# Bound rows read from the accumulator through a picking product; query scalings and unhurried norm applications on GpSimd

## The chip, the core and the metric

The kernel runs on one core of a Trainium2 chip. The metric is device time in microseconds (us) of one execution. A core has five engines that run their own instruction streams and wait for each other through semaphores: TensorE (PE, matrix products into PSUM; PEld is its weight load), ScalarE (ACT, activation functions), VectorE (DVE), GpSimd (POOL) and SyncE (SP, which issues the transfers).

## The reference: what is computed

Two transformer layers over 2048 tokens of width 512, each an attention with 32 heads of width 16, and a feed-forward block of width 1376. The layers share their weights.

```python
def _A_ref(x, wqkv, wo):            # attention, H = 32, Dh = 16
    qkv = ...(x @ wqkv)...
    scores = jnp.einsum("bhqd,bhkd->bhqk", q, k) * Dh ** -0.5
    p = _softmax(scores, axis=-1)
    o = jnp.einsum("bhqk,bhkd->bhqd", p, v)
    return (...o...) @ wo

def _B_ref(x, w1, b1, w2, b2):      # feed-forward, F = 1376
    y = _layernorm(x, axis=-1)
    h = _gelu(jnp.einsum("bsd,df->bsf", y, w1) + b1)
    return jnp.einsum("bsf,fd->bsd", h, w2) + b2

x = A_x                              # (1, 2048, 512)
x = x + _A_ref(_layernorm(x), A_wqkv, A_wo)
x = x + _B_ref(_layernorm(x), B_w1, B_b1, B_w2, B_b2)
x = x + _A_ref(_layernorm(x), A_wqkv, A_wo)
x = x + _B_ref(_layernorm(x), B_w1, B_b1, B_w2, B_b2)
```

## The kernel before

The kernel is a Python program that makes a static schedule: jobs (generators) hand in tasks for an engine, a list scheduler with a duration for every task puts them in order, and the order found is emitted as five instruction streams. The code's layer numbers are 1 and 3.

Attention is cut into 88 *segments*. A segment is one group of four heads (`hg`, 8 of them) and one group of query tokens (512 wide, the last two groups of the second layer 256). A segment's work is score tiles of 128 keys x 512 queries for each head. The first query group of each layer is split into two segments by key blocks (`nparts == 2`), so that it can begin before all keys are there: 32 segments are of this kind. In the first eight segments (the narrow stage) only ACT takes the exponentials.

The exponential of a score is taken with a bound instead of the row maximum. The bound stands in row 16 of each head's 32 rows in the query block `QT`, which is made by one multiply-and-add with a scale per row and a bias:

```python
def job_qt(self, sg, s):
    q = yield ("get", "qt")                       # one of three query slots
    yield ("keys", [("scl", L, part)])
    yield Task("dve", 0.4, [I(lambda e: e.tensor_scalar(out=self.QT[:, q, 0:W], in0=src,
        scalar1=self.scl[:, k, hg:hg + 1], scalar2=self.qbias[:, 0:1], op0=ALU.mult, op1=ALU.add), ...)])
    ...
```

The exponential of a tile is taken in one of two ways. ACT takes groups of three and two tiles with its Exp. DVE takes single tiles: it converts the score to an integer whose bits are a bf16 power of two (`d_load`), and three added shifts of it, multiplied by four scaled copies of the values, make up the exponential:

```python
def d_load(self, d):                              # L1466: PSUM to integer bits
    ... Task("dve", 0.0, [I(lambda e: e.tensor_scalar(out=self.dp[:, u, w * 512:(w + 1) * 512],
            in0=self.ps[:, b, :], scalar1=BITS0, scalar2=None, op0=ALU.add), ...)])

def job_d(self, bt):                              # L1497: three shifts for two tiles
    for k in range(1, len(SHIFT)):
        yield Task("dve", pr, [I(lambda e, k=k, v=v: e.tensor_scalar(out=self.dp[:, v, 0:N],
            in0=self.dp[:, u, 0:N], scalar1=float(SHIFT[k]), scalar2=None, op0=ALU.add), ...)])
```

Which tiles DVE takes is not fixed. Five of the sixteen key blocks (`DK`) may go to it, and `take_d` gives it one when its queue is short; what it does not take goes to ACT:

```python
def take_d(self, hps):
    if ... self.dload > 1 or P.free["dve"] - S_.now > 1.3 or sum(o[4] for t in S_.pend["dve"] for o in t.ops) > DBACK:
        return None
    if self.batch is None and (not S_.pools["dp"].free or ... or self.flying >= DFLY):
        return None
    ...
```

The products with the values are accumulated in one PSUM bank, `ACCB`, 17 rows for each of four heads (16 values and the sum). At a segment's end DVE transposes the bank. For a split segment the two parts have different bounds, so their bounds are needed too: DVE transposes the query block for it.

```python
def job_segend(self, sg):
    yield Task("dve", 0.3, [... e.transpose(self.accT[:, a, 0:W], self.ps[:, ACCB, 0:W]) ...])     # L1593
    T = self.accT[:, a, 0:W].rearrange("p (b r) -> p b r", r=32)
    if nparts == 2:
        xs = yield ("get", "xn")
        rowT = self.xn[:, xs, :].rearrange("p (b r) -> p b r", r=32)
        yield Task("dve", 1.2, [... e.transpose(self.xn[:, xs, :], self.QT[:, q, :]) ...])         # L1602
    S_.release("qt", q)
    if nparts == 2 and part == 0:
        yield Task("dve", 1.2, [... e.tensor_copy(out=self.rowA[:, hg, :], in_=rowT[:, :, 16]) ...])
        ...                                       # GpSimd keeps values and sums of part 0
        return
    if nparts == 2:
        yield Task("dve", 1.2, [... e.tensor_tensor(out=dw, in0=rowT[:, :, 16], in1=self.rowA[:, hg, :], op=ALU.subtract) ...])
        yield Task("act", -1.0, [... exp of dw ...])
        yield Task("pool", 1.2, [... part 0 rescaled and added, four tensor_tensor ...])           # L1621 to L1624
    ...
```

A norm takes its statistics on DVE, the inverse root on GpSimd, and is applied on DVE (`xn` has three slots, shared with the transposed query block):

```python
def ln_apply(self, tt, slot, i, dst, dres, prio):
    c = 4 * slot + i
    return Task("dve", prio, [I(lambda e: e.tensor_scalar(out=dst, in0=self.xres[:, tt, :],
        scalar1=self.mv[:, c, 0:1], scalar2=self.rs[:, c:c + 1], op0=ALU.subtract, op1=ALU.mult), ...)])   # L859
```

It is called for the first four tiles of the first layer, for keys and queries of the others (twice for tiles 4 to 15 of the first layer, once in the second), and for the input of the feed-forward blocks. GpSimd also makes the scaled values `vs` of a segment (L1157) and the norms of queries.

After scheduling, gaps of PE are filled with products by zero (`zw`; L1295, L1297, L1299).

Of the kernel before, what the change touches and what calls it, by code (L numbers as in the profile page):

```python
# [511 lines left out]
class Builder:  # L512
# [171 lines left out]
    def build_startup(self):  # L684
# [155 lines left out]

    def ln_group(self, tiles, slot, prio, eps1, eps0):

# [11 lines left out]
        yield Task("pool", prio, [I(lambda e: e.tensor_scalar(out=rs, in0=var, scalar1=eps1, scalar2=eps0, op0=ALU.mult, op1=ALU.add), [("mv", c0 + i) for i in range(n)], [R], 0.2)])  # L854
        yield Task("pool", prio, [I(lambda e: e.tensor_tensor(out=rs, in0=rs, in1=self.cneg[:, 0:n], op=ALU.pow), [R, ("cneg",)], [R], 0.45 + 0.15 * n)])

    def ln_apply(self, tt, slot, i, dst, dres, prio):
        c = 4 * slot + i
        return Task("dve", prio, [I(lambda e: e.tensor_scalar(out=dst, in0=self.xres[:, tt, :], scalar1=self.mv[:, c, 0:1], scalar2=self.rs[:, c:c + 1], op0=ALU.subtract, op1=ALU.mult),  # L859
                                    [("x", tt), ("mv", c), ("rs", slot)], [dres], 0.395, (), "fast")])  # L860
# [263 lines left out]
    def job_qt(self, sg, s):  # L1124
# [6 lines left out]
        src, RS = (self.psbf(self.q0bank)[:, 0:512], ("ps", self.q0bank)) if s is None else (self.qraw[:, s, 0:W], ("qraw", s))  # L1131
        yield Task("dve", 0.4, [I(lambda e: e.tensor_scalar(out=self.QT[:, q, 0:W], in0=src, scalar1=self.scl[:, k, hg:hg + 1], scalar2=self.qbias[:, 0:1], op0=ALU.mult, op1=ALU.add),
                                  [RS, ("scl", k), ("qbias",)], [("qt", q)], 0.16 + 0.24 * W / 512, (), "fast")])
        if s is None:
# [451 lines left out]
    def job_segend(self, sg):  # L1586
# [10 lines left out]
        T = self.accT[:, a, 0:W].rearrange("p (b r) -> p b r", r=32)  # L1597
        if nparts == 2:
            xs = yield ("get", "xn")
            RX = ("xn", xs)  # L1600
            rowT = self.xn[:, xs, :].rearrange("p (b r) -> p b r", r=32)
            yield Task("dve", 1.2, [I(lambda e: e.transpose(self.xn[:, xs, :], self.QT[:, q, :]), [("qt", q)], [RX], 0.68)])  # L1602
        S_.release("qt", q)
# [3 lines left out]
        if nparts == 2 and part == 0:  # L1607
            yield Task("dve", 1.2, [I(lambda e: e.tensor_copy(out=self.rowA[:, hg, :], in_=rowT[:, :, 16]), [RX], [("rowA", hg)], 0.17)])
            S_.release("xn", xs)
            if L == 3:  # L1610
# [4 lines left out]
        if nparts == 2:
            dw = self.dw[:, hg % 2, :]
            RW = ("dw", hg % 2)
            yield Task("dve", 1.2, [I(lambda e: e.tensor_tensor(out=dw, in0=rowT[:, :, 16], in1=self.rowA[:, hg, :], op=ALU.subtract), [RX, ("rowA", hg)], [RW], 0.17)])
            S_.release("xn", xs)
            yield Task("act", -1.0, [I(lambda e: e.activation(out=dw, in_=dw, func=ACTF.Exp, scale=EXPS), [RW], [RW], 0.23)])  # L1620
# [309 lines left out]
```

## Time and profile before

The median of three runs is 1602.28 us (1602.15 to 1602.88). The profiled execution spans 1601.8 us, at full granted TensorE clock throughout.

| what | number |
|---|---|
| DVE score conversions (L1466) | 921 |
| DVE shifts (L1497) | 1410 |
| ACT exponential groups (L1374) | 1283, of 3 tiles (609) or 2 tiles (674) |
| DVE query scalings (L1132) | 88 |
| DVE norm applications (L859) | 74 |
| DVE transposes of the query block (L1602) | 32 |
| GpSimd instructions | 406 |

In a line of the groups, the first part is line, engine, operation and output<-input; after xcount come busy us and mean ns of one, and after the second bar the idle time of the engine just before these instructions with what ended it. Instructions of one engine overlap a little, so the sum of a group's durations exceeds the time that it blocks its engine.

### The profile page before, as it was taken

The numbers are of one execution on the slowest core, as the hardware profiler recorded it, in microseconds if no ns is written. First come the engines' busy times: TensorE is split into PE (matmuls) and PEld (weight loads), VectorE is DVE, ScalarE is ACT, GpSimd is POOL, SyncE is SP. The second block draws the span as 40 slices with busy tenths as digits, with TensorE's granted clock in tenths as the row PEclk, the third lists the DMA queues.
The fourth block names the chain that finished last, engine by engine and source line by source line (L and its number), as shares of the span: only waits on it lengthen the run. The fifth ranks groups of instructions, "written<-read, shape, count | busy, mean of one in ns | idle before, by whom it ended". The sixth has DMA issues, their size and how long they took to land.

```text
span 1601.8 us, 39236 instructions
## 1 busy us (share of the span) xinstructions
PE 1571.1 (98%) x16532; PEld 481.3 (30%) x16532; DVE 1473.8 (92%) x3323; ACT 1535.5 (96%) x1366; POOL 207.0 (13%) x406
## 2 busy tenths in 40 slices
PE   9999999999999999999999999999999999999998
PEld 3222222222222222222222233222222222344454
DVE  7999999999999899989999899999899989998893
ACT  6999999999999999989999989999999999999995
POOL 4464210000200001001211124300000000000000
PEclk9999999999999999999999999999999999999999
DMA  6671011213321122222822232210101100211100
GB/s 168 122 168 63 22 31 31 53 30 76 84 44 46 36 62 80 56 61 77 138 45 64 58 71 67 60 26 21 31 15 37 31 22 18 40 40 40 41 22 20
DMA packets 212464, 88.79 MB, mean 55 GB/s; under 512 B 183835, under 2 KB 206656, under 8 KB 212288
## 3 DMA queue, kind: packets, MB, share of 16 engines
q1 hardware_dynamic: 212288, 86.29, 24.0%
q8 instruction: 129, 2.11, 0.6%
q14 instruction: 47, 0.39, 0.1%
HBM read 34.65 MB, written 19.48 MB: 34 GB/s over the span
## 4 chain that ended last, share of the span: by engine, by line
PE 49%; ACT 28%; DVE 20%; issue 1%; DMA 1%; POOL 1%; POOLq 0%; DVEq 0%
ACT PT L1374 25%; PE ps L1389 17%; PE ps L1563 14%; DVE dp L1466 7%; DVE dp L1497 5%; PE ps L1747 4%; PE ps L1704 4%; PE ps L916 4%; PE ps L1295 3%; ACT h L1739 2%; PE ps L1299 1%; DVE accT L1593 1%; PE ps L1297 1%; DVE st L846 1%; PE ps L1649 1%
## 5 line engine op out<-in xcount | busy, mean ns | idle before, releaser
L1374 ACT ACTIVATE PT<-ps 128x1024 bf16<-128x1024 f32 (+1 forms) x1283 | 1457.1, 1269 | 36.0 <-PE ps L1389 30.1
L1389 PE MATMUL ps<-QT,KT 32*128 32x512 bf16 (+1 forms) x4608 | 672.5, 358 | 11.5 <-DVE dp L1466 2.2
L1466 DVE TENSOR_SCALAR dp<-ps 128x512 uint16<-128x512 f32 x921 | 618.7, 683 | 56.7 <-PE ps L1389 54.0
L1497 DVE TENSOR_SCALAR dp<-dp 128x1024 uint16<-128x1024 uint16 (+1 forms) x1410 | 533.0, 421 | 7.4 <-PE ps L1563 3.3
L1563 PE MATMUL ps<-PT,V 128*17 128x512 bf16 (+1 forms) x3568 | 468.3, 358 | 0.0
L1563 PE MATMUL ps<-dp,vs 128*17 128x512 bf16 (+1 forms) x3120 | 441.0, 357 | 0.7 <-DVE dp L1497 0.6
L1389 PEld LDWEIGHTS ps<-QT,KT 32*128 32x128 bf16 x4608 | 169.9, 91 | 541.8 <-ACT PT L1374 260.4
L1563 PE MATMUL ps<-dp,V 128*17 128x512 bf16 (+1 forms) x1040 | 214.5, 357 | 2.3 <-DVE accT L1593 2.0
L1297 PE MATMUL ps<-zw 32*128 32x444 bf16 (+2 forms) x714 | 197.6, 325 | 0.0
L1563 PEld LDWEIGHTS ps<-dp,vs 128*17 128x17 bf16 x3120 | 110.9, 88 | 125.1 <-issue 100.9
L1563 PEld LDWEIGHTS ps<-PT,V 128*17 128x17 bf16 x3568 | 112.3, 88 | 105.3 <-issue 94.4
L1299 PE MATMUL ps<-zw 128*32 128x448 bf16 (+23 forms) x1621 | 142.6, 318 | 0.7 <-DVE dp L1466 0.6
L1295 PE MATMUL ps<-zw 128*128 128x448 bf16 (+17 forms) x560 | 130.6, 334 | 4.1 <-DVE dp L1466 2.2
L854 POOL TENSOR_SCALAR rs<-mv 128x4 f32<-128x4 f32 (+2 forms) x19 | 6.6, 347 | 879.1 <-DVE mv L847 877.7
L1704 PE MATMUL ps<-yT,wf 128*128 128x512 bf16 (+3 forms) x396 | 103.5, 360 | 1.0 <-DVE yT L1830 0.5
L916 PE MATMUL ps<-wqkv,xnT 128*128 128x512 bf16 x336 | 93.1, 382 | 1.0 <-DVE h L929 0.5
L1157 POOL TENSOR_SCALAR vs<-V 128x340 bf16<-128x340 bf16 (+2 forms) x72 | 60.5, 841 | 139.7 <-PE ps L1563 121.6
L1295 PEld LDWEIGHTS ps<-zw 128*128 128x128 bf16 x560 | 42.9, 98 | 83.5 <-issue 52.7
L1563 PEld LDWEIGHTS ps<-dp,V 128*17 128x17 bf16 x1040 | 51.3, 88 | 53.1 <-issue 28.5
L1728 DVE TENSOR_SCALAR h<-ps,b1c 128x512 bf16<-128x512 f32 (+2 forms) x88 | 62.3, 708 | 1.8 <-PE ps L1704 1.5
L1593 DVE STREAM_TRANSPOSE accT<-ps 128x512 f32<-128x512 f32 (+1 forms) x88 | 58.1, 660 | 6.1 <-PE ps L1563 4.9
L1299 PEld LDWEIGHTS ps<-zw 128*32 128x32 bf16 x1621 | 52.4, 95 | 24.7 <-DVE dp L1466 5.7
(172 smaller groups left out, 903.0 us busy)
## 6 DMA issues: line engine op xcount, KB each, us to landing
vs<-vs_scr SPq DMA_DIRECT2D x56, 255.0 KB, 2.7
wf<-in_B_w_dram SPq DMA_DIRECT2D x90, 128.0 KB, 2.8
q_scr<-qk SPq DMA_DIRECT2D x22, 256.0 KB, 2.4
k_scr<-qk SPq DMA_DIRECT2D x12, 256.0 KB, 2.3
out_dram<-xres SPq DMA_DIRECT2D x16, 128.0 KB, 1.7
vs_scr<-vs SPq DMA_DIRECT2D x8, 255.0 KB, 3.8
xres<-in_A_x_dram SPq DMA_DIRECT2D x7, 256.0 KB, 3.1
v_scr<-vst SPq DMA_DIRECT2D x12, 136.0 KB, 1.8
```

The costliest lines, as they stand in the source:

```text
L916: yield Task("pe", prio, [I(lambda e, c=c: e.matmul(self.ps[:, b, :], lhsT=xnT[:, c, :], rhs=self.wqkv[:, c, which * 512:which * 512 + 512 ...
L1295: fn = lambda e: e.matmul(self.ps[:, b, 0:w], lhsT=self.zw[:, 0:128], rhs=self.zw[:, 0:w], start=st, stop=st, skip_group_check=True)
L1297: fn = lambda e: e.matmul(self.ps[:, b, 0:w], lhsT=self.zw[32 * p:32 * p + 32, 0:128], rhs=self.zw[32 * p:32 * p + 32, 0:w], start=st, sto ...
L1299: fn = lambda e: e.matmul(self.ps[32 * p:32 * p + 32, b, 0:w], lhsT=self.zw[:, 0:32], rhs=self.zw[:, 0:w], start=st, stop=st, skip_group_c ...
L1374: S_.submit(Task("act", 1e-5 * gi, [I(lambda e, pt=pt, n=n, b0=b0: e.activation(out=self.PT[:, pt:pt + n, :], in_=self.ps[:, b0:b0 + n, :] ...
L1389: return [I(lambda e, kb=kb, i=i: e.matmul(self.ps[:, b, i * W:(i + 1) * W], lhsT=self.KT[32 * hp:32 * hp + 32, hg, kb * 128:(kb + 1) * 12 ...
L1466: self.S_.submit(Task("dve", 0.0, [I(lambda e: e.tensor_scalar(out=self.dp[:, u, w * 512:(w + 1) * 512], in0=self.ps[:, b, :], scalar1=BIT ...
L1497: yield Task("dve", pr, [I(lambda e, k=k, v=v: e.tensor_scalar(out=self.dp[:, v, 0:N], in0=self.dp[:, u, 0:N], scalar1=float(SHIFT[k]), sc ...
L1563: ops.append((nth[j, sh] + 0.1 * i, I(lambda e, hp=hp, v=v, ap=ap[:, i * W:(i + 1) * W], first=first and i == 0, W=W: e.matmul(self.ps[32 ...
L1593: yield Task("dve", 0.3, [I(lambda e: e.transpose(self.accT[:, a, 0:W], self.ps[:, ACCB, 0:W]), [("ps", ACCB)], [RA], 0.17 + 0.535 * W / 5 ...
L1704: yield Task("pe", pr, [I(lambda e, c=c: e.matmul(self.ps[0:M, b, off:off + W], lhsT=self.w1(fc, c), rhs=self.yT[:, c, 0:W], start=(c == 0 ...
L1747: yield Task("pe", pr, [I(lambda e, fc=fc, i=i, b=b: e.matmul(self.ps[:, b, :], lhsT=self.gt(fc, i, W), rhs=self.w2(L, fc), start=(fc == 0 ...
```

## The change

It has three parts, all of them there to take work off DVE.

The bound row comes out of the accumulator. For the 32 split segments a first product, with a matrix `rsel` that holds a single one for each head, copies row 16 of the head's query rows to row 17 of the head's accumulator rows. It opens the accumulation in the place of the first value product. The transpose of the accumulator, which DVE does anyway, then brings the row along, and the transpose of the query block falls away.

The query scalings go to GpSimd from the fifth segment on, with the same multiply and add.

The norm applications that are not hurried go to GpSimd. For this the norm is written as multiply and add: a new column `nmr` = -(mean x inverse root) is made by two small GpSimd instructions per norm group. Tiles 0 to 3 of the first layer, tiles 12 to 15 of both layers' attention inputs, and tiles 12 to 15 of the first layer's feed-forward inputs stay on DVE.

```diff
@@ consts
+            yield dve(lambda e: e.memset(self.rsel[:, :, :], 0.0), [], [("rsel",)], 0.1)
+            yield dve(lambda e: e.tensor_copy(out=self.rsel[:, :, 17], in_=self.iogt[:, :]), [("iogt",)], [("rsel",)], 0.1)
@@ ln_group
+        if shift:
+            nmr = self.nmr[:, c0:c0 + n]
+            yield Task("pool", prio, [I(lambda e: e.tensor_tensor(out=nmr, in0=self.mv[:, c0:c0 + n, 0], in1=rs, op=ALU.mult), ...),
+                                      I(lambda e: e.tensor_scalar(out=nmr, in0=nmr, scalar1=-1.0, scalar2=None, op0=ALU.mult), ...)])
@@ ln_apply
+        if eng == "pool":
+            return Task("pool", prio, [I(lambda e: e.tensor_scalar(out=dst, in0=self.xres[:, tt, :], scalar1=self.rs[:, c:c + 1], scalar2=self.nmr[:, c:c + 1], op0=ALU.mult, op1=ALU.add),
+                                         [("x", tt), ("nmr", slot), ("rs", slot)], [dres], 0.92, (), 0.09)])
@@ job_qkv_tile
-        yield self.ln_apply(tt, slot, i, xnr, RX, prio)
+        yield self.ln_apply(tt, slot, i, xnr, RX, prio, "dve" if tt >= 12 else "pool")
@@ job_yt
-        yield self.ln_apply(tt, slot, i, self.xn[:, xr, :], ("xn", xr), pr - 1)
+        yield self.ln_apply(tt, slot, i, self.xn[:, xr, :], ("xn", xr), pr - 1, "dve" if L == 1 and tt >= 12 else "pool")
@@ job_qt
-        yield Task("dve", 0.4, [... QT ..., 0.16 + 0.24 * W / 512, (), "fast")])
+        eng = "dve" if sg["i"] < 4 else "pool"
+        yield Task(eng, 0.4, [... QT ..., 0.16 + 0.24 * W / 512 if eng == "dve" else 0.41 + 0.48 * W / 512, (), "fast" if eng == "dve" else 0.09)])
@@ try_pv
+                if first and sg["nparts"] == 2:
+                    first = False
+                    ops.append((nth[j, sh] - 0.1, I(lambda e, hp=hp, q=q: e.matmul(self.ps[32 * hp:32 * hp + 18, ACCB, :], lhsT=self.rsel[:, hp, :], rhs=self.QT[:, q, :], start=True, stop=False, ...))))
@@ job_segend
-        if nparts == 2:
-            xs = yield ("get", "xn")
-            rowT = self.xn[:, xs, :].rearrange("p (b r) -> p b r", r=32)
-            yield Task("dve", 1.2, [I(lambda e: e.transpose(self.xn[:, xs, :], self.QT[:, q, :]), [("qt", q)], [RX], 0.68)])
...
-            yield Task("dve", 1.2, [... e.tensor_copy(out=self.rowA[:, hg, :], in_=rowT[:, :, 16]) ...])
+            yield Task("dve", 1.2, [... e.tensor_copy(out=self.rowA[:, hg, :], in_=T[:, :, 17]) ...])
...
-            yield Task("dve", 1.2, [... e.tensor_tensor(out=dw, in0=rowT[:, :, 16], in1=self.rowA[:, hg, :], op=ALU.subtract) ...])
+            yield Task("dve", 1.2, [... e.tensor_tensor(out=dw, in0=T[:, :, 17], in1=self.rowA[:, hg, :], op=ALU.subtract) ...])
```

The last entries of a GpSimd task (0.09) say by how much the scheduler lengthens a DVE instruction marked "fast" that overlaps it.

More of the change, by code (lines that the diff above doesn't have):

```diff
@@ L575, in alloc @@
         self.sel = t("sel", [32, 128], BF16)
+        self.rsel = t("rsel", [128, 4, 18], BF16)
         self.onesm = t("onesm", [128, 1], F32)
@@ L615, in alloc @@
         self.rs = t("rs", [128, 16], F32)
+        self.nmr = t("nmr", [128, 16], F32)
         self.ioi = self.dp[:, 6, 0:256].bitcast(F32)
@@ L838, in flow_weights, with ln_group @@
                 S_.mark(("w2", 3, qc, fc))
-    def ln_group(self, tiles, slot, prio, eps1, eps0):
+    def ln_group(self, tiles, slot, prio, eps1, eps0, shift):
         for i, tt in enumerate(tiles):
@@ L855, in ln_group, with ln_apply @@
         yield Task("pool", prio, [I(lambda e: e.tensor_tensor(out=rs, in0=rs, in1=self.cneg[:, 0:n], op=ALU.pow), [R, ("cneg",)], [R], 0.45 + 0.15 * n)])
-    def ln_apply(self, tt, slot, i, dst, dres, prio):
+        if shift:
+            nmr = self.nmr[:, c0:c0 + n]
+            yield Task("pool", prio, [I(lambda e: e.tensor_tensor(out=nmr, in0=self.mv[:, c0:c0 + n, 0], in1=rs, op=ALU.mult), [R] + [("mv", c0 + i) for i in range(n)], [("nmr", slot)], 0.2),
+                                      I(lambda e: e.tensor_scalar(out=nmr, in0=nmr, scalar1=-1.0, scalar2=None, op0=ALU.mult), [("nmr", slot)], [("nmr", slot)], 0.2)])
+    def ln_apply(self, tt, slot, i, dst, dres, prio, eng="dve"):
         c = 4 * slot + i
+        if eng == "pool":
+            return Task("pool", prio, [I(lambda e: e.tensor_scalar(out=dst, in0=self.xres[:, tt, :], scalar1=self.rs[:, c:c + 1], scalar2=self.nmr[:, c:c + 1], op0=ALU.mult, op1=ALU.add),
+                                         [("x", tt), ("nmr", slot), ("rs", slot)], [dres], 0.92, (), 0.09)])
         return Task("dve", prio, [I(lambda e: e.tensor_scalar(out=dst, in0=self.xres[:, tt, :], scalar1=self.mv[:, c, 0:1], scalar2=self.rs[:, c:c + 1], op0=ALU.subtract, op1=ALU.mult),
@@ L869, in job_lnqkv @@
         slot = yield ("get", "lnc")
-        yield from self.ln_group(tiles, slot, prio, 1.0, EPS)
+        yield from self.ln_group(tiles, slot, prio, 1.0, EPS, tiles[0] >= 4 or L == 3)
         left = [len(tiles) * (1 if later is None else 2)]
@@ L1131, in job_qt @@
         src, RS = (self.psbf(self.q0bank)[:, 0:512], ("ps", self.q0bank)) if s is None else (self.qraw[:, s, 0:W], ("qraw", s))
-        yield Task("dve", 0.4, [I(lambda e: e.tensor_scalar(out=self.QT[:, q, 0:W], in0=src, scalar1=self.scl[:, k, hg:hg + 1], scalar2=self.qbias[:, 0:1], op0=ALU.mult, op1=ALU.add),
-                                  [RS, ("scl", k), ("qbias",)], [("qt", q)], 0.16 + 0.24 * W / 512, (), "fast")])
+        eng = "dve" if sg["i"] < 4 else "pool"
+        yield Task(eng, 0.4, [I(lambda e: e.tensor_scalar(out=self.QT[:, q, 0:W], in0=src, scalar1=self.scl[:, k, hg:hg + 1], scalar2=self.qbias[:, 0:1], op0=ALU.mult, op1=ALU.add),
+                                  [RS, ("scl", k), ("qbias",)], [("qt", q)], 0.16 + 0.24 * W / 512 if eng == "dve" else 0.41 + 0.48 * W / 512, (), "fast" if eng == "dve" else 0.09)])
         if s is None:
@@ L1556, in try_pv @@
                 sg["first"].add(hp)
+                if first and sg["nparts"] == 2:
+                    first = False
+                    ops.append((nth[j, sh] - 0.1, I(lambda e, hp=hp, q=q: e.matmul(self.ps[32 * hp:32 * hp + 18, ACCB, :], lhsT=self.rsel[:, hp, :], rhs=self.QT[:, q, :], start=True, stop=False, skip_group_check=True, tile_position=(0, 32 * hp)),
+                                                     [("rsel",), ("qt", q)], [("ps", ACCB)], W / 2400.0, [("ps", ACCB)], ("col", hp))))
                 for i, kb in enumerate(kbs):
@@ L1597, in job_segend @@
         T = self.accT[:, a, 0:W].rearrange("p (b r) -> p b r", r=32)
-        if nparts == 2:
-            xs = yield ("get", "xn")
-            RX = ("xn", xs)
-            rowT = self.xn[:, xs, :].rearrange("p (b r) -> p b r", r=32)
-            yield Task("dve", 1.2, [I(lambda e: e.transpose(self.xn[:, xs, :], self.QT[:, q, :]), [("qt", q)], [RX], 0.68)])
         S_.release("qt", q)
@@ L1607, in job_segend @@
         if nparts == 2 and part == 0:
-            yield Task("dve", 1.2, [I(lambda e: e.tensor_copy(out=self.rowA[:, hg, :], in_=rowT[:, :, 16]), [RX], [("rowA", hg)], 0.17)])
-            S_.release("xn", xs)
+            yield Task("dve", 1.2, [I(lambda e: e.tensor_copy(out=self.rowA[:, hg, :], in_=T[:, :, 17]), [RA], [("rowA", hg)], 0.17)])
             if L == 3:
@@ L1617, in job_segend @@
             RW = ("dw", hg % 2)
-            yield Task("dve", 1.2, [I(lambda e: e.tensor_tensor(out=dw, in0=rowT[:, :, 16], in1=self.rowA[:, hg, :], op=ALU.subtract), [RX, ("rowA", hg)], [RW], 0.17)])
-            S_.release("xn", xs)
+            yield Task("dve", 1.2, [I(lambda e: e.tensor_tensor(out=dw, in0=T[:, :, 17], in1=self.rowA[:, hg, :], op=ALU.subtract), [RA, ("rowA", hg)], [RW], 0.17)])
             yield Task("act", -1.0, [I(lambda e: e.activation(out=dw, in_=dw, func=ACTF.Exp, scale=EXPS), [RW], [RW], 0.23)])
@@ L1677, in job_post @@
         slot = yield ("get", "lnc")
-        yield from self.ln_group(tiles, slot, pr - 1, 1.0 + EPS, EPS * EPS)
+        yield from self.ln_group(tiles, slot, pr - 1, 1.0 + EPS, EPS * EPS, True)
         if self.prev(L, qc):
```

## The prediction

> **What bounds the kernel now.** I read the head of the page first, then its costliest groups.
>
> ```profile
> PE 1571.1 (98%) x16532; PEld 481.3 (30%) x16532; DVE 1473.8 (92%) x3323; ACT 1535.5 (96%) x1366; POOL 207.0 (13%) x406
> ...
> L1374 ACT ACTIVATE PT<-ps 128x1024 bf16<-128x1024 f32 (+1 forms) x1283 | 1457.1, 1269 | 36.0 <-PE ps L1389 30.1
> L1389 PE MATMUL ps<-QT,KT 32*128 32x512 bf16 (+1 forms) x4608 | 672.5, 358 | 11.5 <-DVE dp L1466 2.2
> L1466 DVE TENSOR_SCALAR dp<-ps 128x512 uint16<-128x512 f32 x921 | 618.7, 683 | 56.7 <-PE ps L1389 54.0
> L1497 DVE TENSOR_SCALAR dp<-dp 128x1024 uint16<-128x1024 uint16 (+1 forms) x1410 | 533.0, 421 | 7.4 <-PE ps L1563 3.3
> ```
>
> The busy PE is not the limit: the groups of `zw` (L1295, L1297, L1299: 130.6, 197.6 and 142.6 us) are multiplications by zero that fill its gaps. The limit is the exponentials. There are 4096 score tiles of 128x512 (2 layers x 32 heads x 16 key blocks x 4 query groups of 512). DVE took 921 of them (L1466 x921, then three bit shifts, L1497); ACT took the other 3175, which costs it 1457.1 / 3175 = 0.459 us a tile. ACT idles 1601.8 - 1535.5 = 66 us. So the time moves when tiles move from ACT to DVE, and the builder's scheduler moves them by itself: `take_d` takes a tile whenever DVE's backlog is short. Up to 5 of 16 key blocks may go, 1280 - 32 = 1248 tiles outside the first, narrow stage; 921 is far from that cap. What limits DVE's share is DVE's time.
>
> Then windows by stage (columns: stretch, its length, busy us of PE, PEld, DVE, ACT, POOL, then clock, DMA share, GB/s):
>
> ```profile
> 0.00:100.00 100.00, 95.96 (x632) 31.81 (x633) 85.29 (x193) 80.86 (x92) 48.95 (x105) 1.00 0.66 143
> 100.00:250.00 150.00, 146.31 (x1582) 42.45 (x1584) 146.89 (x334) 148.74 (x139) 47.36 (x95) 1.00 0.25 61
> 250.00:740.00 490.00, 485.00 (x4540) 129.46 (x4533) 454.33 (x1011) 480.68 (x413) 27.51 (x52) 1.00 0.23 55
> 740.00:950.00 210.00, 207.31 (x1952) 57.11 (x1951) 199.66 (x442) 204.31 (x176) 38.53 (x73) 1.00 0.38 75
> 950.00:1050.00 100.00, 97.41 (x1018) 30.32 (x1017) 96.72 (x220) 91.45 (x88) 37.26 (x70) 1.00 0.28 64
> 1050.00:1550.00 500.00, 493.68 (x6260) 166.78 (x6255) 465.88 (x1067) 495.87 (x427) 5.91 (x8) 1.00 0.13 31
> ```
>
> ACT is 98 to 99% busy nearly everywhere after 100 us, and DVE is full (98%) from 100 to 250 and 97% from 950 to 1050, but at 93% in the long stretches. Only the first 100 us and the last 25 have real holes on ACT. GpSimd is nearly empty after 250 except in the layer change.
>
> The DVE and GpSimd groups, shapes kept apart, give what is to be moved:
>
> ```profile
> L859 DVE TENSOR_SCALAR xn<-xres,mv,rs 128x512 bf16<-128x512 bf16 x70 | 27.7, 428 | 3.8 <-POOL rs L855 2.8 <-DMA xnT<-xn 0.3 <-DMA yT<-xn 0.2
> L1132 DVE TENSOR_SCALAR QT<-qraw,scl,qbias 128x512 bf16<-128x512 bf16 x71 | 28.7, 406 | 0.4
> L1602 DVE STREAM_TRANSPOSE xn<-QT 128x512 bf16<-128x512 bf16 x32 | 22.0, 686 | 0.7 <-DMA xnT<-xn 0.7
> L1132 DVE TENSOR_SCALAR QT<-qraw,scl,qbias 128x256 bf16<-128x256 bf16 x16 | 5.0, 313 | 0.0
> ...
> L1157 POOL TENSOR_SCALAR vs<-V 128x340 bf16<-128x340 bf16 x24 | 26.0, 1084 | 31.2 <-PE ps L1563 30.0
> ```
>
> Last, the timeline around a GpSimd burst (start, us, what): the shift of 0.42 us takes 0.71 us beside a GpSimd multiplication (POOL L1621 at 188.20), and a scaling 0.46 beside L1157.
>
> ```profile
> 184.00 0.42 DVE L1497 TENSOR_SCALAR dp<-dp 128x1024 uint16<-128x1024 uint16 x1
> ...
> 187.33 0.46 DVE L1132 TENSOR_SCALAR QT<-qraw,scl,qbias 128x512 bf16<-128x512 bf16 x1
> ...
> 188.39 0.71 DVE L1497 TENSOR_SCALAR dp<-dp 128x1024 uint16<-128x1024 uint16 x1
> ```
>
> **What the Trainium skill says.** "SBUF — State Buffer" (SBUF: two separate sides) says that VectorE and GpSimd share one pair of ports, as an exclusive lock held for the whole instruction, taken by a VectorE instruction in a two-port mode or with two SBUF inputs. The trace agrees that they disturb each other, but not on the size: beside the 1.08 us GpSimd scalings of L1157 the DVE instructions stretch by some 0.1 us, beside its tensor-by-tensor products by 0.3, and neither waits out the other's length. [...]No run here has a 512-wide GpSimd multiply-and-add yet; L1157, multiply alone, took 1.08 us for 340 elements. The kernel's author enters 0.89 and 0.92 us in the scheduler; I take 0.9 to 1.2 us in company of DVE. "Perfetto Trace Analysis" (Optimizing Scalar/DVE Operations) allows offloading from a saturated DVE, but warns that "offloading operations between those two might not help" because of that lock.
>
> **The change part by part.** Consecutive DVE instructions overlap by about 0.08 us in the trace (two L1466 of 0.68 span 1.25 to 1.29), so what an instruction blocks is its mean less 0.08. By that a DVE tile costs 0.60 + 1.5 x 0.34 = 1.11 us (three shifts serve two tiles).
> - Query scalings: 88 segments, from the fifth on to GpSimd, 84. Outside the narrow stage (first eight segments) 64 of 512 columns and 16 of 256: 64 x 0.326 + 16 x 0.233 = 24.6 us.
> - Norm applications: keys and queries of tiles 4 to 11 in the first layer (8 + 8), tiles 0 to 11 in the second (12), FFN inputs 12 and 14: 54. Eight fall in the narrow stage; 46 x 0.348 = 16.0 us.
> - Transposes of the query block for the bound row: all 32 go; 24 outside the narrow stage, 24 x 0.606 = 14.5 us. In their place come 4 x 32 = 128 products of 18 x 512 on PE, which take the place of filler, and the row is read from the accumulator that DVE transposes anyway.
> - Two small negations per norm group on GpSimd: off any path.
>
> Freed on DVE where it can be turned into tiles: 55 us. Against it, 80 scalings and 46 applications of about 1 us on GpSimd, each meeting about one fast DVE instruction, at 0.1 us: 126 x 0.1 = 13 us. Net 42 us. If x tiles move, DVE must pay 1.11 x out of these 42 us and out of a span shorter by 0.459 x, of which it is busy 94% (1315.6 of 1400 us, 150 to 1550): 1.11 x + 0.43 x = 42, x = 27 tiles, and the time falls by 27 x 0.459 = 12.5 us. The applications were done in stretches where DVE is at 93% already, waiting for scores (the 56.7 us before L1466), so I count half of theirs as unused: 8 / 1.54 x 0.459 = 2.4 us less. In the narrow stage about 9 us of DVE (8 x 0.606 + 4 x 0.326 + 8 x 0.348) are freed, but no tile goes to DVE there; ACT idled 5 us between 50 and 100, of which I credit 1 to 2. Sum: 12.5 - 2.4 + 1.5 = about 12 us, 1602 to 1590.
>
> **The rivals.**
> 1. *The lock costs more than counted.* If each GpSimd instruction holds DVE for 0.3 us, as the products do, 126 x 0.3 = 38 us eat most of the 55, x = 11, gain 5 us: 1597. If DVE truly waited out a length, the kernel would be slower, about 1615. For it: L1497 at 0.71 to 0.94 beside products. Against: L1132 at 0.46 to 0.54 beside L1157, the same kind of instruction as the new ones.
> 2. *GpSimd becomes the bound at the stage changes.* Between 90 and 120 us it is busy 21.4 of 30 us, and queries' norms, the scaled values and now scalings queue there; a late scaling stops a whole segment's scores. Seven or eight applications add 8 us there. For it: that the values of a segment (L1157) gate its DVE tiles. Against: three query slots mean a scaling has about a segment's time (15 to 20 us), and it has the better priority. It would cost 3 to 8 us: about 1597.
> 3. *DVE's freed time stays empty.* Its idle before L1466 ends on a score of PE 87 times, so tiles could be short in supply rather than time. Then only the stretches at 97 to 98% gain, a third of it: 1597.
> 4. *Better than a trade.* Shorter DVE queues also shorten the stage changes (ACT lost 8.5 us between 950 and 1050, 5.7 between 740 and 950): 1580 to 1585.
>
> **Range and chances.** The upper bound of the mechanism is all freed time used and no contention: 55 / 1.54 x 0.459 = 16 us, plus some 5 of rival 4, so below 1580 is hard; 2% would be 1570. Rivals 1 to 3 together take back most, and the static schedule falls out differently at every edit, which I put at 5 us either way. Predicted 1590 us, range 1580 to 1600. Faster by over 2%: 0.05; within 2%: 0.93; slower by over 2%: 0.02.
>
> **What would show it.** Right: L1466's count rises from 921 to about 945 to 955, the count of L1374 falls by some 11 groups, ACT's busy time falls by about 12 us with its share staying at 96%, DVE stays at 92%, GpSimd goes from 13% to about 21%. The moved scalings and applications would show near 1 us each on GpSimd, and L1497's mean of 421 ns rises by 5 to 10 ns. Wrong: L1466's count as before (rival 3), L1497's mean up by 25 ns or more (rival 1), or longer waits of ACT for L1389 in 50 to 150 and 950 to 1050 (rival 2).

## The result and the profile after

The changed kernel takes 1596.34 us (median of 4 runs, 1595.61 to 1597.54) against 1602.22 us (4 runs, 1602.10 to 1602.88): ratio 0.9963, interval 0.9946 to 0.9980. It gained 5.9 us; about 12 were predicted. The time lies inside the range, the gain is half of the forecast.

The head of the page and the costliest groups of the changed kernel (lines have moved: L1386 are ACT's exponentials, L1401 the scores, L1478 and L1509 DVE's conversions and shifts, L1144 the scalings):

```profile
PE 1538.6 (97%) x16364; PEld 479.4 (30%) x16497; DVE 1450.3 (91%) x3202; ACT 1528.0 (96%) x1357; POOL 333.9 (21%) x574
...
L1386 ACT ACTIVATE PT<-ps 128x1536 bf16<-128x1536 f32 (+1 forms) x1274 | 1449.7, 1259 | 38.8 <-PE ps L1401 32.2
L1401 PE MATMUL ps<-QT,KT 32*128 32x512 bf16 (+1 forms) x4608 | 672.3, 358 | 16.8 <-DVE dp L1478 5.5
L1478 DVE TENSOR_SCALAR dp<-ps 128x512 uint16<-128x512 f32 x944 | 632.6, 681 | 61.2 <-PE ps L1401 58.2
L1509 DVE TENSOR_SCALAR dp<-dp 128x1024 uint16<-128x1024 uint16 (+1 forms) x1434 | 557.4, 430 | 7.9 <-PE ps L1579 3.2
```

DVE took 944 tiles in place of 921. ACT's busy time fell by 7.5 us (1535.5 to 1528.0), and DVE's by 23.5 us. The moved work, in the GpSimd groups with shapes kept apart, is all there and as long as assumed:

```profile
L1144 POOL TENSOR_SCALAR QT<-qraw,scl,qbias 128x512 bf16<-128x512 bf16 x68 | 62.1, 914 | 601.9 <-PE ps L1401 596.8 <-DVE scl L1113 5.1
L868 POOL TENSOR_SCALAR xn<-xres,rs,nmr 128x512 bf16<-128x512 bf16 x54 | 50.6, 944 | 6.5 <-DMA yT<-xn 3.5 <-DMA xnT<-xn 1.7
...
L1144 POOL TENSOR_SCALAR QT<-qraw,scl,qbias 128x256 bf16<-128x256 bf16 x16 | 10.1, 633 | 188.0 <-PE ps L1401 188.0
```

The windows by stage, for comparison with those in the prediction:

```profile
0.00:100.00 100.00, 95.46 (x638) 31.17 (x646) 74.29 (x170) 82.50 (x94) 62.96 (x120) 1.00 0.67 145
100.00:250.00 150.00, 143.32 (x1516) 42.11 (x1522) 143.57 (x325) 147.06 (x137) 61.43 (x117) 1.00 0.23 60
250.00:740.00 490.00, 476.24 (x4486) 129.75 (x4538) 455.71 (x986) 477.76 (x409) 72.19 (x108) 1.00 0.23 55
740.00:950.00 210.00, 202.88 (x1939) 57.83 (x1955) 199.67 (x438) 202.99 (x174) 48.70 (x86) 1.00 0.37 76
950.00:1050.00 100.00, 95.94 (x1107) 29.72 (x1108) 94.59 (x212) 94.07 (x91) 46.26 (x82) 1.00 0.26 61
1050.00:1550.00 500.00, 486.93 (x6248) 170.35 (x6291) 463.93 (x1035) 494.99 (x426) 40.84 (x58) 1.00 0.15 31
```

What the reader is to see: from 100 to 950 us ACT is a little *less* busy than before (827.8 us in place of 833.7), and yet no further on. Only at the layer change, 950 to 1050, and at the start is it fuller. The transposes of the accumulator mark the end of each segment in both traces. The 16th segment ends at 234.7 us before and 233.9 after, the 48th at 959.0 and 959.3. Between them DVE took 427 tiles before and 443 after, and the stretch became 1.1 us longer. So 16 more tiles bought nothing there. The 56th segment ends at 1020.2 and 1014.8: behind the layer change the changed kernel is 5.4 us ahead. From there on, 7 more tiles brought another 0.6 us by the last segment.

**Where ACT's saved time went.** ACT's exponentials come in groups of three and two tiles. The spacing from one group's start to the next is 1.331 us (three) and 0.904 us (two) when they run without a break; these are the commonest spacings in both traces. I call what exceeds it a *gap*, and sum it over all neighbouring groups of a trace. The gaps sum to 67.1 us before and 72.4 us after. About half of that shows as idle time of ACT between groups (33.2 and 35.7 us); the busy time hides the other half, because an instruction's duration overlaps the next (a three-tile group lasts 1.43 us at least). At these spacings the groups themselves take 1419.9 us before and 1409.6 after, so the 23 tiles save ACT 10.3 us, and 5.3 us of new gaps take back half of it. The rest of the profiled span lies ahead of the first group (0.9 us less), behind the last (2.4 less) and in ACT's other work between groups (0.5 more). Together that is the 7.7 us between the two profiled spans (1601.8 and 1594.1); the profiled execution before was 1.2 us above its median.

Such a gap looks like this in the timeline of the changed kernel. First ACT, then PE, on which no filler ran here (start, us, what):

```profile
622.91 2.37 ACT L1386 ACTIVATE PT<-ps 128x1536 bf16<-128x1536 f32 x2
625.51 1.45 ACT L1386 ACTIVATE PT<-ps 128x1536 bf16<-128x1536 f32 x1 [0.22 <-PE ps L1401]
```

```profile
623.77 0.81 PE L1658 MATMUL ps<-wo,OT 128*128 128x512 bf16 x3
624.51 0.39 PE L1579 MATMUL ps<-dp,vs 128*17 128x512 bf16 x2
...
624.73 0.38 PE L1579 MATMUL ps<-dp,vs 128*17 128x512 bf16 x2
624.73 0.38 PE L1579 MATMUL ps<-PT,V 128*17 128x512 bf16 x1
625.05 0.90 PE L1401 MATMUL ps<-QT,KT 32*128 32x512 bf16 x6
```

ACT's three-tile group began at 622.91, so its banks came free at about 624.3. Output products (L1658) and value products (L1579) stood ahead in PE's instruction stream, and the next scores began at 625.05. The two-tile group behind it began at 624.24, so the next could have followed at 625.15; ACT began it at 625.51. PE is not full (the products by zero still take 444 us of the changed kernel), but a batch begun at the wrong moment makes the next scores late.

### The profile page after: what moved, and what is told of

Its sections match the earlier page's. It is cut to its first block, busy times and chain, and to the rows that moved or that the text cites. A ratio compares the mean times of both kernels' runs of the same rounds, so it can differ in the third digit from the quotient of the medians.

```text
span 1594.1 us, 39159 instructions
## 1 busy us (share of the span) xinstructions
PE 1538.6 (97%) x16364; PEld 479.4 (30%) x16497; DVE 1450.3 (91%) x3202; ACT 1528.0 (96%) x1357; POOL 333.9 (21%) x574
## 4 chain that ended last, share of the span: by engine, by line
PE 51%; DVE 28%; ACT 17%; issue 2%; POOL 0%; DMA 0%; POOLq 0%; DVEq 0%
PE ps L1401 18%; ACT PT L1386 15%; PE ps L1579 15%; DVE dp L1478 12%; DVE dp L1509 9%; PE ps L1713 4%; PE ps L1756 4%; PE ps L927 3%; PE ps L1307 3%; ACT h L1748 1%; PE ps L1311 1%; PE ps L1658 1%; DVE accT L1609 1%; DVE st L850 1%; DVE n L992 1%
## 5 line engine op out<-in xcount | busy, mean ns | idle before, releaser
L1386 ACT ACTIVATE PT<-ps 128x1536 bf16<-128x1536 f32 (+1 forms) x1274 | 1449.7, 1259 | 38.8 <-PE ps L1401 32.2
L1401 PE MATMUL ps<-QT,KT 32*128 32x512 bf16 (+1 forms) x4608 | 672.3, 358 | 16.8 <-DVE dp L1478 5.5
L1478 DVE TENSOR_SCALAR dp<-ps 128x512 uint16<-128x512 f32 x944 | 632.6, 681 | 61.2 <-PE ps L1401 58.2
L1509 DVE TENSOR_SCALAR dp<-dp 128x1024 uint16<-128x1024 uint16 (+1 forms) x1434 | 557.4, 430 | 7.9 <-PE ps L1579 3.2
L1579 PE MATMUL ps<-PT,V 128*17 128x512 bf16 (+1 forms) x3544 | 467.1, 358 | 0.0
L1579 PE MATMUL ps<-dp,vs 128*17 128x512 bf16 (+1 forms) x3192 | 444.4, 357 | 0.5 <-DVE dp L1509 0.2
L1401 PEld LDWEIGHTS ps<-QT,KT 32*128 32x128 bf16 x4608 | 172.2, 91 | 546.4 <-ACT PT L1386 237.3
L1144 POOL TENSOR_SCALAR QT<-qraw,scl,qbias 128x512 bf16<-128x512 bf16 (+1 forms) x84 | 72.2, 860 | 790.0 <-PE ps L1401 784.8
L1579 PE MATMUL ps<-dp,V 128*17 128x512 bf16 (+1 forms) x1064 | 215.3, 357 | 1.3 <-DVE accT L1609 1.0
L1309 PE MATMUL ps<-zw 32*128 32x444 bf16 (+5 forms) x702 | 193.5, 323 | 0.0
L1579 PEld LDWEIGHTS ps<-dp,vs 128*17 128x17 bf16 x3192 | 111.0, 88 | 130.3 <-issue 106.8
L1579 PEld LDWEIGHTS ps<-PT,V 128*17 128x17 bf16 x3544 | 113.2, 88 | 102.5 <-issue 89.6
L1311 PE MATMUL ps<-zw 128*32 128x448 bf16 (+22 forms) x1477 | 136.5, 323 | 0.4 <-DVE dp L1478 0.2
L1307 PE MATMUL ps<-zw 128*128 128x448 bf16 (+17 forms) x481 | 114.1, 333 | 4.0 <-DVE ps L727 1.7
L1713 PE MATMUL ps<-yT,wf 128*128 128x512 bf16 (+3 forms) x353 | 92.9, 356 | 8.6 <-issue 4.4
L927 PE MATMUL ps<-wqkv,xnT 128*128 128x512 bf16 x299 | 85.8, 382 | 7.6 <-issue 3.5
L1579 PEld LDWEIGHTS ps<-dp,V 128*17 128x17 bf16 x1064 | 53.1, 88 | 45.2 <-issue 27.3
L1307 PEld LDWEIGHTS ps<-zw 128*128 128x128 bf16 x481 | 37.4, 98 | 74.2 <-issue 46.4
```

Source lines behind the costliest of these rows:

```text
L927: yield Task("pe", prio, [I(lambda e, c=c: e.matmul(self.ps[:, b, :], lhsT=xnT[:, c, :], rhs=self.wqkv[:, c, which * 512:which * 512 + 512 ...
L1144: yield Task(eng, 0.4, [I(lambda e: e.tensor_scalar(out=self.QT[:, q, 0:W], in0=src, scalar1=self.scl[:, k, hg:hg + 1], scalar2=self.qbias ...
L1307: fn = lambda e: e.matmul(self.ps[:, b, 0:w], lhsT=self.zw[:, 0:128], rhs=self.zw[:, 0:w], start=st, stop=st, skip_group_check=True)
L1309: fn = lambda e: e.matmul(self.ps[:, b, 0:w], lhsT=self.zw[32 * p:32 * p + 32, 0:128], rhs=self.zw[32 * p:32 * p + 32, 0:w], start=st, sto ...
L1311: fn = lambda e: e.matmul(self.ps[32 * p:32 * p + 32, b, 0:w], lhsT=self.zw[:, 0:32], rhs=self.zw[:, 0:w], start=st, stop=st, skip_group_c ...
L1386: S_.submit(Task("act", 1e-5 * gi, [I(lambda e, pt=pt, n=n, b0=b0: e.activation(out=self.PT[:, pt:pt + n, :], in_=self.ps[:, b0:b0 + n, :] ...
```

## The experiments

Times are medians. "Tiles" are the conversions on DVE and "gaps" the sum just described, both counted in the profiled execution of each run. In the traces of pick_only, ln_only, null_after4 and after_hold2 the granted TensorE clock is half for 3 to 10 us, and 4.6 to 6.0 us of their gaps fall there. (The expectations put the gaps of the kernel before at 64 us; by the count used here they are 67.1.)

| run | time us | ratio to the kernel before (interval) | tiles | gaps us |
|---|---|---|---|---|
| the kernel before | 1602.22 | | 921 | 67.1 |
| the changed kernel | 1596.34 | 0.9963 (0.9946 to 0.9980) | 944 | 72.4 |
| pick_only | 1598.73 | 0.9977 (0.9966 to 0.9988) | 923 | 65.7 |
| qt_only | 1609.32 | 1.0040 (1.0025 to 1.0055) | 935 | 74.1 |
| ln_only | 1601.94 | 0.9995 (0.9986 to 1.0004) | 923 | 71.3 |
| null_before | 1610.50 | 1.0050 (1.0035 to 1.0065) | 923 | 75.2 |
| null_before2 | 1601.21 | 0.9990 (0.9984 to 0.9997) | 922 | 69.5 |
| null_before3 | 1606.70 | 1.0037 (1.0021 to 1.0053) | 928 | 71.4 |
| null_before4 | 1603.10 | 1.0001 (0.9993 to 1.0010) | 918 | 70.7 |
| null_after1 | 1610.61 | 1.0061 (1.0043 to 1.0079) | 940 | 84.1 |
| null_after2 | 1593.31 | 0.9946 (0.9931 to 0.9961) | 952 | 73.5 |
| null_after3 | 1595.58 | 0.9954 (0.9939 to 0.9969) | 944 | 71.2 |
| null_after4 | 1606.13 | 1.0020 (1.0012 to 1.0028) | 941 | 83.5 |
| dummy_pool | 1622.89 | 1.0122 (1.0107 to 1.0137) | 921 | 86.4 |
| after_fewer_tiles | 1593.24 | 0.9938 (0.9923 to 0.9953) | 924 | 61.4 |
| before_hold | 1593.09 | 0.9936 (0.9921 to 0.9951) | 912 | 56.2 |
| after_hold | 1595.49 | 0.9960 (0.9941 to 0.9979) | 921 | 57.1 |
| before_hold15 | 1590.47 | 0.9926 (0.9911 to 0.9941) | 904 | 51.0 |
| pick_hold15 | 1593.58 | 0.9952 (0.9933 to 0.9971) | 916 | 56.6 |
| after_hold2 | 1590.82 | 0.9929 (0.9914 to 0.9944) | 930 | 64.3 |

Two theories went into the runs. *Tiles decide*: every tile that DVE takes saves ACT's 0.459 us. The rival, *order decides*: what the order of PE does to ACT's gaps outweighs a few tiles, and any edit redraws that order. Over the 20 traces of the table the profiled span goes with the gaps (correlation 0.82) and hardly with the number of tiles (0.11).

### One part at a time

pick_only leaves only the picking product in:

```diff
-        eng = "dve" if sg["i"] < 4 else "pool"        # job_qt
+        eng = "dve"
-        yield self.ln_apply(..., "dve" if tt >= 12 else "pool")      # and the other call
+        yield self.ln_apply(..., "dve")
```

> The kernel before with the picking product alone. Theory of the prediction (every freed us of DVE becomes tiles, every tile is worth 0.459 us): 14.5 us freed, about 9 tiles (930), about 4 us plus 1 to 2 in the narrow stage: 1596 to 1598. Rival, the draw of the schedule (any edit reorders the greedy schedule and moves the time by several us whatever it frees): the tile count says little of the time; anywhere from 1592 to 1608. A third theory, that the gain came from the shorter path at a segment's end and not from tiles: few tiles, but 1594 to 1597, with the layer change from 950 to 1020 us shorter.

1598.7 us with 923 tiles: 3.7 us gained and only 2 tiles more. That is nearly the first theory's time, but without its tiles. The third theory, a shorter path at a segment's end, had 1594 to 1597; the 56th segment does end 3.7 us earlier than in the kernel before (1016.5), but so it does in null_before3 below (1017.2), where that path is as it was.

qt_only leaves only the scalings on GpSimd: the transposes of the query block are back, the norms are applied on DVE.

```diff
-                if first and sg["nparts"] == 2:       # try_pv: no picking product; job_segend as before
+                if False:
-        yield self.ln_apply(..., "dve" if tt >= 12 else "pool")      # and the other call
+        yield self.ln_apply(..., "dve")
```

> The kernel before with the query scalings on GpSimd alone. Theory of the prediction: 24.6 us freed less 80 x 0.1 for contention, 11 tiles (932), 5 us: 1597. Draw of the schedule: tiles rise by about 11, the time lies anywhere from 1594 to 1610. Third theory (path at the segment's end): tiles rise, the time stays at 1601 to 1603.

14 tiles more, and 7 us *slower* than the kernel before. The tiles came in full number and their time did not; the gaps rose by 7.0 us. It speaks against "every tile is worth 0.459 us", though one run cannot end it: the next section shows what a redrawn order alone can do.

ln_only leaves only the norm applications on GpSimd.

```diff
-                if first and sg["nparts"] == 2:       # try_pv: no picking product; job_segend as before
+                if False:
-        eng = "dve" if sg["i"] < 4 else "pool"        # job_qt
+        eng = "dve"
```

> The kernel before with the norm applications on GpSimd alone. Theory of the prediction: 16.0 us freed less 46 x 0.1, half unused, 4 to 7 tiles (925 to 928), 2 to 3 us: 1599 to 1600. Draw of the schedule: few tiles, the time anywhere from 1594 to 1610. Third theory: 1601 to 1603.

1601.9 us, 2 tiles more, no measurable difference, which the second theory and the third both allow. The kernel before stood at 1602.44 beside these three, so the parts are worth -3.7, +6.9 and -0.5 us. Their sum is 2.7 us slower; the whole is 5.9 faster. The parts do not add up.

### Edits that change no work

One number of the scheduler is changed by a few thousandths, its guess for the length of a DVE conversion. It stands in no instruction. Only the order in which the list scheduler lays the tasks differs, and with it the few tiles that fall to the other engine (918 to 928 on DVE for the kernel before, 940 to 952 for the changed one). I call such an order a *draw*. The guesses were not taken blind: the first four runs were taken where the builder's own layout lay far from that of the original guess, to either side, and the later four fill up pairs.

```diff
-    [("ps", b)], [("dp", u, w)] + self.dres(u), 0.682)]),
+    [("ps", b)], [("dp", u, w)] + self.dres(u), 0.678)]),      # or 0.681, 0.683, 0.684
```

> The kernel before with no work added, removed or moved: only the scheduler's guess for one DVE conversion is 0.678 us in place of 0.682, so ties in the order fall differently. Theory of the prediction: the same tiles and the same time within 1 us, 1601 to 1603. Draw of the schedule: tiles within 5 of 921, the time off by 3 to 8 us.

1610.5 us, 8 us slower, with 923 tiles.

> The kernel before with no work altered: the guess is 0.681 us in place of 0.682. One worth: 1601 to 1603. Draw of the schedule: off by 2 to 6 us, here to the fast side.

1601.2 us: 1 us faster, less than the draw had promised.

> The changed kernel with no work altered: the scheduler's guess for one DVE conversion is 0.681 us in place of 0.682. If the change has one worth, the time is that of the changed kernel, 1595 to 1598, with about 944 tiles. If the order that the greedy schedule falls into decides several us, the tiles are about 940 and the time is off by 5 to 10 us, here to the slow side.

1610.6 us: the changed kernel loses its gain and 8 us more, with 940 tiles and gaps of 84.1 us.

> The changed kernel with no work altered: the guess is 0.684 us in place of 0.682. One worth: 1595 to 1598. Draw of the schedule: off by 3 to 7 us, here to the fast side, 1589 to 1594, with 945 to 955 tiles.

1593.3 us, 952 tiles.

> The kernel before, work unaltered, guess 0.683 us: one more draw of the schedule, for a mean over draws. One worth: 1601 to 1604. Draws: 1597 to 1612.

1606.7 us.

> The changed kernel, work unaltered, guess 0.683 us, the partner of the run ahead. One worth: 1595 to 1598. Draws: 1588 to 1612; over the pairs the changed kernel ahead by 5 to 12 us if its tiles count in the mean, by under 4 us if they do not.

1595.6 us.

> The kernel before, work unaltered, guess 0.684 us, the partner of the changed kernel's draw at 0.684 (1593.3). One worth: 1601 to 1604. Draws: 1597 to 1612.

1603.1 us.

> The changed kernel, work unaltered, guess 0.678 us, the partner of the first null edit of the kernel before (1610.5). One worth: 1595 to 1598. Draws: 1588 to 1612.

1606.1 us.

At equal guesses the changed kernel stands against the kernel before like this: 0.678: -4.4 us, 0.681: +9.4, 0.682 (the shipped pair): -5.9, 0.683: -11.1, 0.684: -9.8. The mean is -4.4 us with a standard deviation of 8.2, so for five pairs an interval of about 10 us either way. The draw of the schedule is as large as the effect. A gain near the measured one is the best guess, but neither 0 nor the predicted 12 is excluded as the worth of the change apart from its draw. In the means of five draws each, the changed kernel has 944 tiles against 922 and gaps of 76.9 us against 70.8: 22 tiles at 0.444 us (1.331 / 3) save ACT 9.8 us, and 6.1 us go into gaps. The gaps of single draws spread from 67.1 to 75.2 and from 71.2 to 84.1, so this rise is likely and not certain.

### Contention alone

dummy_pool keeps the kernel before. After its scheduling it sets 138 idle multiply-and-adds on GpSimd behind the scalings and applications that the change would have moved, which stay on DVE as well. ACT and DVE run the same instructions in the same order as before; the zero products that fill PE fell out slightly differently (16546 weight loads of PE in place of 16532). The idle instructions wait for nothing, so GpSimd runs them as soon as it comes to them, often several in a row.

```diff
+            if op.eng == "dve" and (writes "qt", or "xn" from the residual):     # from the 5th and 17th on
+                P.op("pool", lambda e: e.tensor_scalar(out=self.junk[:, :], in0=self.junk[:, :], scalar1=self.onesm[:, 0:1],
+                     scalar2=self.qbias[:, 0:1], op0=ALU.mult, op1=ALU.add), ..., 0.9, 0.0)
```

> The kernel before with its order unchanged on ACT, DVE and SP, and 138 idle 128x512 bf16 multiply-and-adds in place on GpSimd, after the scalings and applications that the change moves (which stay on DVE too): contention alone. Prediction's term: 138 x 0.1 = 14 us of DVE time in all, seen as longer shifts (mean up by some 7 to 10 ns), the time up by 2 to 5 us where it lies on the path. Rival of the heavy lock: 0.3 each, 40 us, shifts up by 25 ns or more, the time up by 8 us or more.

It costs 20 us, four times the upper end of what I expected; the rival, at 0.3 us for each, had 8 us or more. The head of its page and its groups:

```profile
PE 1556.0 (96%) x16410; PEld 482.2 (30%) x16546; DVE 1495.6 (92%) x3323; ACT 1539.2 (95%) x1366; POOL 334.4 (21%) x545
...
L1506 DVE TENSOR_SCALAR dp<-dp 128x1024 uint16<-128x1024 uint16 (+1 forms) x1410 | 540.2, 424 | 6.3 <-PE ps L1572 2.5
```

```profile
L860 DVE TENSOR_SCALAR xn<-xres,mv,rs 128x512 bf16<-128x512 bf16 x70 | 37.1, 561 | 2.6 <-POOL rs L856 1.7 <-DMA xnT<-xn 0.5
...
L1290 POOL TENSOR_SCALAR junk<-junk,onesm,qbias 128x512 bf16<-128x512 bf16 x138 | 131.8, 955 | 8.3
```

DVE's busy time rose by 21.8 us (1473.8 to 1495.6) for the same 3323 instructions, 0.16 us for each idle GpSimd instruction. It is lost beside them: from one start to the next, with waits left out, the 349 DVE instructions that an idle instruction overlaps took 22.2 us more than the same instructions of the kernel before, and all others together 0.3 us less. Shifts lost 10.3 us of it and applications 9.2; the applications as a group went from 428 to 561 ns. DVE's waits on GpSimd did not grow (7.8 us in all in both traces), so it was not GpSimd's queue. ACT's gaps rose by 19.4 us, as much as the profiled span (19.6). In this fixed order DVE's loss lies on the path almost to the full.

### Fewer tiles, and a sharper hold on PE

after_fewer_tiles is the changed kernel with a smaller backlog allowed to DVE before it is given a tile:

```diff
-DBACK = 2.0
+DBACK = 1.0
```

> The changed kernel, but DVE may take a score tile only while its backlog is below 1.0 us in place of 2.0: about 924 tiles, 20 fewer, with DVE's freed time left partly unused. If a tile at the margin is worth 0.459 us, the time is 1596.3 + 9 = 1605. If a tile at the margin is worth next to nothing, because its products delay the scores that ACT waits for, the time is 1590 to 1600, and ACT's gaps between exponential groups are 8 us or more below the changed kernel's.

20 tiles fewer, and 1593.2 us in place of 1596.3. *Tiles decide* had 1605. The gaps are 61.4 us, 11.0 lower and below those of all five draws of the changed kernel; the time is level with the fastest of these draws (null_after2, 1593.3).

before_hold is the kernel before, with nothing moved. The scheduler passes over a PE task if it would delay the coming scores by more than `HOLD_LATE`:

```diff
-HOLD_LATE = 0.4
+HOLD_LATE = 0.2
```

> The kernel before, nothing moved to GpSimd, but the scheduler holds back a PE task that would delay the next scores by over 0.2 us (0.4 before): some 912 tiles, 9 fewer. If tiles decide, 1602 + 4 = 1606. If the gaps between ACT's groups decide, they fall by 10 us or more and the time falls to 1588 to 1596 without any offloading.

1593.1 us, with 912 tiles and gaps of 56.2 us. An edit that moves nothing off DVE gains 9.6 us (1602.7 beside it), more than the change under study, and lies 8 us below the fastest of the five draws of the kernel before.

after_hold puts a sharper hold on the changed kernel, and the next three runs vary the same three constants:

```diff
-HOLD_LATE = 0.4
+HOLD_LATE = 0.25
-DBACK = 2.0
+DBACK = 1.6
-    [("ps", b)], [("dp", u, w)] + self.dres(u), 0.682)]),
+    [("ps", b)], [("dp", u, w)] + self.dres(u), 0.684)]),
```

> The changed kernel with a sharper hold on PE (0.25 us in place of 0.4), a backlog bound of 1.6 in place of 2.0 and the guess 0.684 for a conversion: about 921 tiles, as many as before the change. If tiles decide, 1602 or more. If gaps decide, ACT's gaps are 15 us or more below the changed kernel's and the time is 1583 to 1592, below both kernels.

Its median is 1595.5 us, outside what *order decides* gave; its ten executions run from 1588.8 us at a granted TensorE clock of 1.000 to 1603.4 at 0.990, longer the lower the clock, and why the clock dipped was not tried. The profiled one (1589.9 us) has gaps of 57.1 us.

before_hold15 is the kernel before with `HOLD_LATE` 0.15, `DBACK` 1.6 and guess 0.680; pick_hold15 the picking product alone with 0.15, 1.6 and 0.678; after_hold2 the whole change with 0.25, 1.3 and 0.682.

> The kernel before, nothing moved, with a hold of 0.15 us in place of 0.4, a backlog bound of 1.6 in place of 2.0 and the guess 0.680: about 904 tiles, 17 fewer. If tiles decide, 1602 + 8 = 1610. If the gaps between ACT's groups decide, they lie 15 us or more below the 64 us of the kernel before and the time is 1586 to 1593.

1590.5 us, the fastest kernel of the study by its median, with the fewest tiles and the smallest gaps (51.0 us, 16.1 below the kernel before). It beats both kernels, and differs from the kernel before in three constants. Its page:

```profile
PE 1531.2 (96%) x16123; PEld 474.1 (30%) x16270; DVE 1456.7 (92%) x3282; ACT 1532.7 (97%) x1373; POOL 198.7 (13%) x406
...
L1374 ACT ACTIVATE PT<-ps 128x1024 bf16<-128x1024 f32 (+1 forms) x1290 | 1454.9, 1302 | 29.6 <-PE ps L1389 27.8
L1466 DVE TENSOR_SCALAR dp<-ps 128x512 uint16<-128x512 f32 x904 | 607.2, 681 | 62.1 <-PE ps L1389 59.6
```

ACT has 7 groups more than in the kernel before and is 2.8 us less busy by the page, and the span is 14.7 us shorter. The mean of a group is *longer* (1302 ns against 1269), because more groups follow the one before them without a break: in the kernel before, three-tile groups that start behind a gap of over 60 ns last 1.456 us on average and the others 1.509; here they are 104 in place of 182.

> The picking product alone with the same hold of 0.15 us, bound 1.6, guess 0.678: about 916 tiles and no new instruction on GpSimd. If the picking product is worth its freed DVE time and brings no contention, 2 to 5 us below the run with the hold alone; if gaps decide, within 2 us of it.

1593.6 us: no gain over the hold alone, 3 us slower at that, which neither theory had and which is within what draws do.

> The whole change with a hold of 0.25, bound 1.3, guess 0.682: about 930 tiles. If offloading pays once the gaps are held down, 4 us or more below the run with the hold alone; if contention on GpSimd's side eats it, level with it or slower, 1588 to 1596.

1590.8 us, level with the hold alone. With a sharper hold in both, the offloading shows no worth: 26 more tiles (930 against 904) save ACT 11.7 us, and the gaps are 13.3 us larger (64.3 against 51.0). The two kernels differ in their constants as well and are one draw each, so a worth of some us could hide here.

## Why the prediction was off by half

**What bounds the kernel: right, but read too coarsely.** ACT's exponentials are the bound. I read "98 to 99% busy" as full. The gaps came to 67.1 us, half of them hidden in the overlap of neighbouring groups. The mean duration shows such waiting too: it fell where the gaps grew (1269 to 1259 ns after the change) and rose where they shrank (1302 ns in before_hold15), for groups of either size:

```profile
L1374 ACT ACTIVATE PT<-ps 128x1536 bf16<-128x1536 f32 x609 | 909.0, 1493 | 23.6 <-PE ps L1389 17.8
L1374 ACT ACTIVATE PT<-ps 128x1024 bf16<-128x1024 f32 x674 | 713.1, 1066 | 12.4 <-PE ps L1389 12.3
```

```profile
L1386 ACT ACTIVATE PT<-ps 128x1536 bf16<-128x1536 f32 x605 | 897.1, 1483 | 21.0 <-PE ps L1401 14.9
L1386 ACT ACTIVATE PT<-ps 128x1024 bf16<-128x1024 f32 x668 | 700.8, 1057 | 17.8 <-PE ps L1401 17.4
```

The first two lines are the kernel before, the other two the changed one.

**The freed DVE time: right.** The counts are as worked out: 84 scalings, 54 applications and 32 transposes are gone from DVE. At their mean less 0.08 us they are 32 x 0.606 + 68 x 0.326 + 16 x 0.233 + 54 x 0.348 = 64.1 us over the whole kernel, and 23 tiles at 1.11 us put back 25.5. DVE's busy time should have fallen by 38.6 us; it fell by 23.5.

**Contention: right in size, wrong in place.** The 15 us that DVE did not give up compare with the 13 I set. The wide shifts alone, compared with those that overlap no GpSimd instruction, lost 23.4 us after and 9.9 before, 13.5 more. Their group's mean went from 421 to 430 ns, within the 5 to 10 ns expected. I let this loss only reduce the number of tiles. dummy_pool shows that in a fixed order such a loss can go into the time nearly one for one. How much of it did so in the changed kernel, whose scheduler reckons with 0.09 us for each, was not measured apart.

**The tiles: nearly right.** 27 were worked out, 23 came (22 in the mean of the draws).

**The step that failed** is "x = 27 tiles, and the time falls by 27 x 0.459 = 12.5 us". It takes ACT's time for a tile as the kernel's, and so the gaps between ACT's groups as fixed. With 23 tiles it would still be 10.6 us. ACT was indeed spared 10.3 us, but its gaps grew by 5.3. qt_only has 14 more tiles and is 7 us slower; after_fewer_tiles has 20 fewer than the changed kernel and is 3 us faster. That PE's order sets the gaps is shown by the holds: in before_hold the one constant altered says which PE task may go first; the gaps fell by 10.9 us and the time by 9.6, both below every draw of the kernel before. Nor is it that fewer tiles went to DVE: after_hold has the 921 tiles of the kernel before and 10.0 us less of gaps. What raised the gaps in the changed kernel stays open between three causes: the additional tiles, DVE's loss beside GpSimd, and the draw. For the tiles speaks that a DVE tile needs four value products in place of one, and that in the changed kernel the gaps over 60 ns (from 100 to 1550 us) whose late scores came right after a value product sum to 29.7 us in place of 25.4. But the two traces also differ in their whole order.

**The draw of the schedule**, which I put at 5 us either way, is larger: the same work ran from 1601.2 to 1610.5 us before and from 1593.3 to 1610.6 after. The shipped pair is one pair out of many; its difference of 5.9 us cannot be told from the mean of the pairs, nor from luck.

**The rivals.** A heavier lock (1): not in the shifts' mean, yet dummy_pool's 0.16 us for each instruction lies between my 0.1 and its 0.3. GpSimd as the bound at the stage changes (2): fell, ACT is fuller from 950 to 1050 than before (94.07 in place of 91.45). Freed time left empty (3): fell as stated, since 23 tiles came; but its idea, that PE does not deliver, was the right one, for ACT's scores and not for DVE's. Shorter stage changes (4): came. The changed kernel is 2.0 us ahead at the end of the narrow stage, 0.3 behind at the 48th segment's end, and 5.4 ahead at the end of the layer change, nearly the whole measured gain. The null edits move the same layer change by as much (from the 40th to the 56th segment's end it took 210.0 us before, 203.1 after, and 213.8 in null_after1), so it is not shown to be the change's own.

## What to carry to other kernels

When work is moved from one nearly full engine to another, price it by what starts late because of it, not by the busy time it frees: look at the spacing of the bound engine's instructions, not at its busy share. Where a scheduler lays out the program, make a few edits that change no work before believing a gain of under 1%. And if the bound engine waits for products that stand behind others in PE's stream, try the order first: here three constants of the scheduler, the best of the settings tried, gave 12 us, twice what 170 instructions moved or removed gave.

## What was not expected of the hardware

GpSimd multiply-and-adds of 128x512 bf16 that nobody waits for cost DVE 0.16 us of busy time each (21.8 us for 138) and the kernel 20 us. Which instructions pay could be read because the order on DVE was the same in both traces. The 143 shifts that an idle instruction overlapped lost 0.07 us on average and up to 0.54, the 44 applications 0.21 and up to 0.47, both from SBUF to SBUF; the 88 conversions, which read PSUM, lost nothing (at most 0.008). The shifts' mean hides this: it moved by 3 ns only, and the shifts that met no GpSimd instruction read 4 ns shorter in that trace (419 to 415 ns). The Trainium skill ("SBUF — State Buffer", SBUF: two separate sides) has the loser of the shared ports block for the whole of the other's instruction. The shortest idle instruction lasts 0.757 us and the largest loss seen is 0.54, so no wait of a full length shows here; an instruction that comes midway would wait for the rest alone, and these runs cannot tell that from a lighter lock.
